# Linear attention and two mixtures of experts on one core: first k-v tails and queries behind all k and v on one queue, the four pairs in banks of their own

## The chip, the cores and the metric

One core of a Trainium2 chip runs the whole program. Its engines are TensorE (PE, with its weight loads shown as PEld), VectorE (DVE), ScalarE (ACT), GpSimd (POOL) and SyncE (SP, which here only issues transfers). The metric is the device time of one execution in microseconds; less is better. Every time below is from one profiled execution on the chip, unless it is called a median.

## What is computed

Three stages follow each other. `B, H, S, DH = 4, 8, 576, 64`, so there are 2304 rows of 512 columns after the first.

```python
kv  = einsum('bhsd,bhse->bhde', k, v)            # per batch and head, 64 x 64
out = einsum('bhsd,bhde->bhse', q, kv)
x   = out / sqrt(mean(out*out, -1) + 1e-6) * g_norm
x   = sum over 4 experts of p[:, e] * (relu(x @ w1[e]) @ w2[e])      # dense, all rows
x   = gate * (relu(x @ w1b[e]) @ w2b[e])         # 8 experts, one per row, chosen by cosine
```

## The kernel before

The work is cut into units of 384 rows (three tiles of 128 rows). Only the opening of the program is touched by the change; it computes the attention for the first unit and for the second batch's k-v product, and then the expert products of the first dense mixture start (`plain_phase`, line 1198; matmuls of line 861).

**The k-v product.** For every batch, eight heads are taken as four pairs (`NP = 4`). A pair's product accumulates over S = 576 rows: 512 of them are the main part (`MAIN`, four products of 128 rows for each head, line 127), the 64 left over are the tail (line 130). `kv_unit` (line 119) does main part and tail of a pair in one PSUM bank named by a tag, and then ScalarE copies the two 64x64 blocks into `kv_bd`, a block-diagonal form (line 133). In the opening all four pairs of batch 0 use the one bank "kv". k and v of a pair come in one transfer each of 256 KB (`load_kv`, line 137), the tails of k and v in one transfer each of 128 KB for all eight heads (`load_tail`, line 113), a query tile of 128 rows in one of 256 KB (`load_q`, line 147).

**The order of the opening** is written out by hand, from line 1043. Each engine works its own instructions in the order of the program, and each issuing engine's transfers go out in that order.

- `heat(14)` (line 1052): fourteen 128x128 products of the identity with itself. They warm TensorE and produce nothing. Each is two instructions.
- `load_tail(0, eng=nc.scalar)`: the two tails of batch 0, issued by ScalarE. Then four `issue()` calls: k and v of the four pairs, on SyncE.
- Query tiles 0, 1 and 2 (line 1062): tile 0 is issued by ScalarE, tiles 1 and 2 by SyncE.
- Behind them on SyncE's queue: the first block of expert weights (w1), the tails of batch 1, k and v of batch 1 (four pairs, into `en_b`), three more weight blocks, `dp` (the routing shares), and query tiles 3 and 4 (line 1084).
- Line 1099: for each pair `kv_unit`, `heat(2)`, and, from the third pair on, `q_first` of a query tile (four transposes at line 162 into PSUM, one copy of 128x512 by VectorE or ScalarE). After the pairs come the third `q_first` and, for each tile, `x_first`: eight products (line 179, a record for each half), a Square on ScalarE (line 1096) and a reduction on VectorE (line 1097).
- `heat(10)` (line 1108), while the root of the mean square is worked out (`rms_start`, `rms_end`). Then pairs 0 and 1 of batch 1 on TensorE, the scaling of x on VectorE (line 1118), the transposes of x (line 224) with their copies (lines 231 and 232), and pairs 2 and 3 of batch 1.
- `plain_phase` runs a list of steps with a planned length each, and beside them fillers that are due at a planned time (`todo`). In the first one, the transposes of query tile 3 (`qt_unit`, through `att([TS])`, due from 4.5) are such a filler.

Of the kernel before, what the change touches and what calls it, by code (L numbers as in the profile page):

```python
# [8 lines left out]
F32 = mybir.dt.float32  # L9
# [11 lines left out]
def attn_moe_moe_kernel(ctx: ExitStack, tc: tile.TileContext, q, k, v, g_norm, dprobs, w1, w2, emb, tau, w1b, w2b, out):  # L21
    nc = tc.nc
    ctx.enter_context(tc.manual_schedule())
    B, H, S, DH = q.shape
# [88 lines left out]
    def load_tail(b, home=None, eng=nc.sync):  # L113
        t = home if home is not None else kv_p.tile([S - MAIN, 2, H, DH], F32, name="kvtail", tag="tail", bufs=1)
        for i, src in enumerate((k, v)):
            eng.dma_start(out=t[:, i], in_=src[b, :, MAIN:S, :].rearrange("h p d -> p h d"))
        tail_raw[b] = t

    def kv_unit(b, pair, tag="kv"):
        early = b == 1  # L120
        r = en_b[:, 2 * pair:2 * pair + 2].rearrange("p i n -> p (i n)") if early else take("kv", b, pair)
        r = r.rearrange("p (i h r d) -> p i h r d", i=2, h=2, d=DH)
        tl = tail_raw[b]
        ps = psp.tile([128, DH], F32, name="pskv", tag=tag)
        for c in range(RC):
            for i in range(2):
                nc.tensor.matmul(out=ps[64 * i:64 * i + 64], lhsT=r[:, 0, i, c], rhs=r[:, 1, i, c], start=(c == 0), stop=False)
        for i in range(2):
            hd = 2 * pair + i
            nc.tensor.matmul(out=ps[64 * i:64 * i + 64], lhsT=tl[:, 0, hd], rhs=tl[:, 1, hd], start=False, stop=True)  # L130
        for i in range(2):
            sl = slice(64 * i, 64 * i + 64)
            nc.scalar.copy(kv_bd[b % 2][sl, pair, sl], ps[sl])
        if b > 1:
            issue()
# [909 lines left out]
    def heat(n, w=warm):  # L1045
        for _ in range(n):
            nc.tensor.matmul(out=w, lhsT=ident, rhs=ident, start=True, stop=True)
# [3 lines left out]

    heat(14)
    load_tail(0, eng=nc.scalar)
    for _ in range(RAW):
        issue()
    Q0 = TS

    def q_first_raw(t):
        return xr.rearrange("p u c n -> p (u c n)")[:, D * t:D * t + D]

    for t in range(Q0):
        load_q(t, nc.sync if t else nc.scalar, q_first_raw(t))
    nc.scalar.activation(out=one, in_=one, func=ACTF.Sqrt)
# [21 lines left out]
    qx = [acc[TS + t].rearrange("p (a n) -> p a n", a=NP) for t in range(Q0)]  # L1085
    px = [psp.tile([128, H, DH], F32, name=f"psx{t}", tag=("x0", "x1", "l20")[t]) for t in range(Q0)]
    ms = st_p.tile([128, TS, H], F32, name="ms3", tag="ms3", bufs=1)
# [5 lines left out]
    def x_first(t):  # L1093
# [3 lines left out]
        nc.vector.tensor_reduce(out=ms[:, t], in_=x_s[t], axis=AX.X, op=ALU.add)  # L1097

    for p in range(NP):
        kv_unit(0, p)  # L1100
        heat(2)
        if p > 1:
            q_first(p - 2)
    for t in range(Q0):
        if t + 2 < Q0:
            q_first(t + 2)
        x_first(t)
    heat(10, psp.tile([128, 128], F32, name="warm2", tag="kv"))
    ri = rms_end(*rms_start(ms, [128, TS, H], "s"))
# [3 lines left out]
    for part in range(3):  # L1113
        w1_direct(0, part, nc.gpsimd)
    for p in range(2):
        kv_unit(1, p, ("kv", "l21")[p])
    for t in range(TS):
        nc.vector.tensor_tensor(out=x_s[t], in0=px[t], in1=ri[:, t].unsqueeze(2).to_broadcast([128, H, DH]), op=ALU.mult)
    for t in range(TS):
        xt_unit(t, ("tp", "l10", "l11")[t], first=True)  # L1120
    for p in range(2, NP):
        kv_unit(1, p, ("kv", "l21")[p - 2])
    issue()
# [70 lines left out]
    todo = w2_fills(0, 0) + [(-1, f) for f in plain_direct(1)]  # L1194
    todo += [(6.0, norm_probs)]
    todo += [(14.2 + 0.4 * c, lambda c=c: nc.vector.tensor_tensor(
# [249 lines left out]
```

## Time and profile before

| what | us |
|---|---|
| median of three runs | 1115.49 |
| lowest and highest run | 1114.94, 1117.86 |
| the profiled execution, whole time | 1114.02 |
| its span in the trace | 1112.2 |
| granted TensorE clock, mean (share of full speed) | 0.999 |
| ScalarE busy in the span | 484.0 (44%) |
| VectorE busy in the span | 626.8 (56%) |

The span runs from the first to the last instruction in the trace; the whole time is 1.8 us longer. A busy time is the time in which an engine has an instruction under way; TensorE's instructions are pipelined, so several records overlap. All moments below are counted from the start of the span.

### The profile page before, as it was taken

How to read it: one execution, taken by the hardware profiler on the slowest of the kernel's cores; microseconds unless marked ns; L12 is line 12 of the kernel's file. 1: busy time of each engine (PE TensorE's matmuls, PEld its weight loads, DVE VectorE, ACT ScalarE, POOL GpSimd, SP SyncE). 2: the span in 40 equal slices, each digit the busy share in tenths (PEclk: the TensorE clock that was granted, in tenths of full speed). 3: DMA queues.
4: the chain of work that ended last, by engine and by line, in shares of the span. 5: the costliest groups of instructions: out<-in, count | busy, mean ns of one | idle time of the engine just before them, and what ended most of it. 6: DMA issues, size and time to landing. Idle time of an engine off the chain costs nothing. (4 is left out here: it accounts for less than half of the span.)

```text
span 1112.2 us, 17150 instructions
## 1 busy us (share of the span) xinstructions
PE 1098.1 (99%) x5894; PEld 965.2 (87%) x5894; DVE 626.8 (56%) x1175; ACT 484.0 (44%) x892; POOL 192.8 (17%) x232
## 2 busy tenths in 40 slices
PE   8999999999999999999999999999999999999997
PEld 8889888998888988899999888889987888888885
DVE  3665564657884455544573555743469683375452
ACT  3644437544454222233333222222366584475562
POOL 3112232321440100000020001010011121112111
PEclk9999999999999999999999999999999999999999
DMA  9736697766878446455465565465473783566471
GB/s 275 239 133 227 265 375 280 259 202 248 307 277 294 168 163 217 153 198 208 166 235 180 213 218 180 171 228 208 152 264 133 245 317 113 197 230 233 160 258 34
DMA packets 91012, 239.86 MB, mean 216 GB/s; under 512 B 19285, under 2 KB 38741, under 8 KB 90784
## 3 DMA queue, kind: packets, MB, share of 16 engines
q1 hardware_dynamic: 81376, 213.71, 54.2%
q0 software_dynamic: 7440, 24.41, 6.5%
q8 instruction: 49, 0.80, 0.3%
q10 hardware_dynamic: 2096, 0.52, 0.2%
q14 instruction: 51, 0.42, 0.1%
HBM read 230.22 MB, written 56.63 MB: 258 GB/s over the span
## 5 line engine op out<-in xcount | busy, mean ns | idle before, releaser
L968 PE MATMUL bank<-w2h,hh 128*128 128x512 f32 x576 | 227.3, 395 | 0.5 <-ACT hh L845 0.5
L968 PE MATMUL bank<-w2l,hh 128*128 128x512 f32 x576 | 225.1, 391 | 0.4 <-DMA w2l<-held_w 0.4
L968 PE MATMUL bank<-w2h,hl 128*128 128x512 f32 x576 | 225.2, 391 | 0.0
L873 PE MATMUL bank<-xth,w1h 128*128 128x384 f32 x616 | 159.6, 340 | 0.4 <-DVE acc L977 0.2
L873 PE MATMUL bank<-xtl,w1h 128*128 128x384 f32 x616 | 156.8, 335 | 0.0
L873 PE MATMUL bank<-xth,w1l 128*128 128x384 f32 x616 | 156.7, 335 | 0.0
L977 DVE SCALAR_TENSOR_TENSOR acc<-bank,dp,acc 128x512 f32<-128x512 f32 x120 | 89.8, 749 | 110.2 <-PE bank L968 110.0
L968 PEld LDWEIGHTS bank<-w2h,hl 128*128 128x128 f32 x576 | 108.1, 188 | 24.0 <-DVE hl L848 1.1
L968 PEld LDWEIGHTS bank<-w2h,hh 128*128 128x128 f32 x576 | 108.2, 188 | 22.8 <-ACT hh L845 1.8
L968 PEld LDWEIGHTS bank<-w2l,hh 128*128 128x128 f32 x576 | 108.2, 188 | 21.8 <-DMA w2l<-held_w 0.8
L873 PEld LDWEIGHTS bank<-xth,w1h 128*128 128x128 f32 x616 | 109.6, 188 | 4.0 <-ACT w1h L60 0.6
L873 PEld LDWEIGHTS bank<-xtl,w1h 128*128 128x128 f32 x616 | 111.5, 188 | 0.0
L873 PEld LDWEIGHTS bank<-xth,w1l 128*128 128x128 f32 x616 | 111.3, 188 | 0.0
L880 ACT COPY s<-bank 128x384 f32<-128x384 f32 x88 | 42.2, 479 | 156.6 <-PE bank L873 156.4
L884 POOL TENSOR_TENSOR sv<-sv,s 128x384 f32<-128x384 f32 x44 | 49.0, 1113 | 348.5 <-ACT sv L880 274.1
L61 DVE TENSOR_TENSOR w2l<-raw,w2h 128x1024 fp32r<-128x1024 f32 x64 | 75.8, 1221 | 23.6 <-ACT w2h L60 23.0
L341 DVE CUSTOM_DVE_ANT_0 scr<-row,en_b 128x512 bf16<-128x512 f32 x96 | 68.4, 713 | 10.7 <-DMA row<-x1d 9.9
L1293 PE MATMUL psy<-w2h,hth 128*128 128x512 f32 x176 | 71.0, 404 | 0.4 <-ACT hth L1284 0.4
L1293 PE MATMUL psy<-w2h,htl 128*128 128x512 f32 x176 | 68.8, 391 | 0.4 <-DVE htl L367 0.4
L1293 PE MATMUL psy<-w2l,hth 128*128 128x512 f32 x176 | 69.0, 392 | 0.0
L60 ACT CAST w2h<-raw 128x1024 fp32r<-128x1024 f32 x64 | 64.6, 1052 | 5.7 <-DMA raw<-in_moe_w_dram 5.3
L61 DVE TENSOR_TENSOR w1l<-raw,w1h 128x256 fp32r<-128x256 f32 (+2 forms) x75 | 55.0, 755 | 14.0 <-ACT w1h L60 13.9
(259 smaller groups left out, 1645.6 us busy)
## 6 DMA issues: line engine op xcount, KB each, us to landing
raw<-in_moe_w_dram SPq DMA_DIRECT2D x224, 512.0 KB
w1h<-held_w SPq DMA_DIRECT2D x28, 896.0 KB
w1l<-held_w SPq DMA_DIRECT2D x28, 896.0 KB
w2h<-held_w SPq DMA_DIRECT2D x34, 512.0 KB
w2l<-held_w SPq DMA_DIRECT2D x34, 512.0 KB
held_w<-w1h SPq DMA_DIRECT2D x16, 896.0 KB
held_w<-w1l SPq DMA_DIRECT2D x16, 896.0 KB
held_w<-w2h SPq DMA_DIRECT2D x16, 512.0 KB
```

What stands on the lines that cost most here:

```text
L60: nc.scalar.copy(hi, raw)
L61: (eng or nc.vector).tensor_tensor(out=lo, in0=raw, in1=hi.bitcast(F32), op=ALU.subtract)
L341: nc.vector.tensor_tensor_reduce(out=scr, in0=x, in1=en_b[:, e], scale=1.0, scalar=0.0, op0=ALU.mult, op1=ALU.add, accum_out=lg[:, t, e:e + 1]
L873: nc.tensor.matmul(out=ps, lhsT=wform(wo, b, w)[:, c], rhs=xform(xo, x)[:, c], start=start and n == 0, stop=(n == 5), skip_group_check=True)
L880: nc.scalar.copy(t, src)
L884: (eng or nc.vector).tensor_tensor(out=out, in0=a, in1=b, op=ALU.add)
L968: nc.tensor.matmul(out=ps, lhsT=h_t[o][f][u][:, ns], rhs=w[j][:, a], start=(k == 0 and m == 0), stop=(k == 3 and m == 2))
L977: nc.vector.scalar_tensor_tensor(out=fin, in0=ps, scalar=dp[:, t, e:e + 1], in1=ac, op0=ALU.mult, op1=ALU.add)
L1293: nc.tensor.matmul(out=ps, lhsT=x[:, f], rhs=w[j][:, o], start=(f == 0 and i == 0), stop=(f == NF - 1 and i == 2))
```

## The change

Both tails of batch 0 and query tile 0 are issued by SyncE, behind all k and v of batch 0. The main parts of the four pairs are computed one after the other, each in a bank of its own, with a `heat` behind each; the four tails, and the copies, follow them, with the copies of pairs 2 and 3 on VectorE. The query tiles' transposes come after that, and the x products of a tile start before the transposes of the next-but-one. There is less warm-up work: 5 in place of 14 at the start, 7 and 1 in place of 8 around the pairs, 4 in place of 10 after x. Pairs 0 and 1 of batch 1 share one bank with a `heat(2)` between them, and pair 3 of batch 1 becomes a filler of the first expert phase, due at 2.1.

```diff
-    def kv_unit(b, pair, tag="kv"):
+    def kv_main(b, pair, tag):
         early = b == 1
         r = en_b[:, 2 * pair:2 * pair + 2].rearrange("p i n -> p (i n)") if early else take("kv", b, pair)
         r = r.rearrange("p (i h r d) -> p i h r d", i=2, h=2, d=DH)
-        tl = tail_raw[b]
         ps = psp.tile([128, DH], F32, name="pskv", tag=tag)
         for c in range(RC):
             for i in range(2):
                 nc.tensor.matmul(out=ps[64 * i:64 * i + 64], lhsT=r[:, 0, i, c], rhs=r[:, 1, i, c], start=(c == 0), stop=False)
+        return ps
+
+    def kv_rest(b, pair, ps, copy=nc.scalar.copy):
+        tl = tail_raw[b]
         for i in range(2):
             hd = 2 * pair + i
             nc.tensor.matmul(out=ps[64 * i:64 * i + 64], lhsT=tl[:, 0, hd], rhs=tl[:, 1, hd], start=False, stop=True)
         for i in range(2):
             sl = slice(64 * i, 64 * i + 64)
-            nc.scalar.copy(kv_bd[b % 2][sl, pair, sl], ps[sl])
+            copy(kv_bd[b % 2][sl, pair, sl], ps[sl])
+
+    def kv_unit(b, pair, tag="kv"):
+        kv_rest(b, pair, kv_main(b, pair, tag))
         if b > 1:
             issue()
...
-    heat(14)
-    load_tail(0, eng=nc.scalar)
+    heat(5)
     for _ in range(RAW):
         issue()
+    load_tail(0)
     Q0 = TS
...
     for t in range(Q0):
-        load_q(t, nc.sync if t else nc.scalar, q_first_raw(t))
+        load_q(t, nc.sync, q_first_raw(t))
...
-    px = [psp.tile([128, H, DH], F32, name=f"psx{t}", tag=("x0", "x1", "l20")[t]) for t in range(Q0)]
...
+    mains = []
     for p in range(NP):
-        kv_unit(0, p)
-        heat(2)
-        if p > 1:
-            q_first(p - 2)
+        mains.append(kv_main(0, p, ("kv", "x0", "x1", "l20")[p]))
+        heat(2 if p + 1 < NP else 1)
+    for p in range(NP):
+        kv_rest(0, p, mains[p], nc.scalar.copy if p < 2 else nc.vector.tensor_copy)
+    px = [psp.tile([128, H, DH], F32, name=f"psx{t}", tag=("x0", "x1", "l20")[t]) for t in range(Q0)]
+    q_first(0)
+    heat(1)
     for t in range(Q0):
-        if t + 2 < Q0:
-            q_first(t + 2)
+        if t + 1 < Q0:
+            q_first(t + 1)
         x_first(t)
-    heat(10, psp.tile([128, 128], F32, name="warm2", tag="kv"))
+    heat(4, psp.tile([128, 128], F32, name="warm2", tag="kv"))
...
-    for p in range(2):
-        kv_unit(1, p, ("kv", "l21")[p])
+    kv_unit(1, 0, "kv")
+    heat(2, psp.tile([128, 128], F32, name="warm2", tag="l21"))
+    kv_unit(1, 1, "kv")
...
-    for p in range(2, NP):
-        kv_unit(1, p, ("kv", "l21")[p - 2])
+    kv_unit(1, 2, "kv")
     issue()
...
-    todo += [(6.0, norm_probs)]
+    todo += [(2.1, lambda: kv_unit(1, 3)), (6.0, norm_probs)]
```

## Rows read from the trace of the kernel before

A row of the timeline gives start, length, engine, line, operation, what it writes and reads, and how many instructions were merged; in brackets stands the idle time before them and what ended it.

**Rows 1.** The page's head and its busy time of each engine.

```profile
span 1112.2 us, 17150 instructions
PE 1098.1 (99%) x5894; PEld 965.2 (87%) x5894; DVE 626.8 (56%) x1175; ACT 484.0 (44%) x892; POOL 192.8 (17%) x232
```

**Rows 2.** Waits of TensorE after 25 us: total, times, longest.

```profile
PE psm L1271 <- DVEq L807: 2.2, 2, 2.0
PE bank L968 <- ACT hh L845: 0.5, 2, 0.4
```

**Rows 3.** Timeline of TensorE in the first 26 us.

```profile
9.48 0.69 PE L127 MATMUL pskv<-raw 128*64 128x64 f32 x16 [1.33 <-DMA raw<-in_v_dram]
10.10 0.33 PE L130 MATMUL pskv<-kvtail 64*64 64x64 f32 x4
10.36 0.71 PE L1047 MATMUL warm<-ident 128*128 128x128 f32 x4
...
14.48 1.04 PE L162 MATMUL psq<-ident,xr 128*128 128x128 f32 x8
15.36 2.84 PE L179 MATMUL psx<-kvbd,acc 128*128 128x128 f32 x24
18.04 2.40 PE L1047 MATMUL warm<-ident 128*128 128x128 f32 x20
...
21.37 0.69 PE L127 MATMUL pskv<-en_b 128*64 128x64 f32 x16
...
22.25 1.55 PE L224 MATMUL psxt<-ident,acc 128*128 128x128 f32 x12
...
25.48 0.97 PE L861 MATMUL bank<-xth,w1h 128*128 128x384 f32 x4
```

**Rows 4.** Timeline of the queues of ScalarE and SyncE: when each transfer is issued.

```profile
0.76 0.71 ACTq L116 DMA_DIRECT2D kvtail<-in_k_dram  x1
...
0.76 0.46 SPq L139 DMA_DIRECT2D raw<-in_k_dram  x1
...
7.06 2.79 SPq L154 DMA_DIRECT2D xr<-in_q_dram  x2
9.96 2.38 SPq L614 DMA_DIRECT2D raw<-in_moe_w_dram  x1
```

**Rows 5.** Windows: PE, PEld, DVE, ACT, POOL busy; PEclk, DMA share, GB/s.

```profile
2.00:5.00 3.00, 3.00 (x16) 3.00 (x16) 0.00 (x0) 1.49 (x2) 1.50 (x3) 1.00 0.98 261
5.00:8.00 3.00, 2.93 (x37) 2.59 (x36) 0.00 (x0) 0.38 (x2) 0.00 (x0) 1.00 0.91 225
8.00:12.00 4.00, 2.64 (x47) 2.08 (x45) 0.00 (x0) 0.45 (x3) 0.00 (x0) 1.00 1.12 349
14.00:20.00 6.00, 6.00 (x55) 6.00 (x55) 2.81 (x5) 3.20 (x8) 0.00 (x0) 1.00 0.97 280
```

**Rows 6.** DMA queues from 5 to 8, 8 to 12 and 12 to 14 us.

```profile
q1 hardware_dynamic: 452, 0.44, 51.3%
q10 hardware_dynamic: 945, 0.24, 39.0%
...
q1 hardware_dynamic: 2082, 1.32, 103.7%
...
DMA packets 1295, 0.46 MB, mean 229 GB/s; under 512 B 1123, under 2 KB 1295, under 8 KB 1295
```

**Rows 7.** Timeline of TensorE's weight loads: transposes of query tile 3.

```profile
32.04 0.42 PEld L162 LDWEIGHTS psq<-ident,qraw 128*128 128x128 f32 x4 [0.37 <-DMA qraw<-in_q_dram]
```

**Rows 8.** Timeline of VectorE: first query copy, and the scaling of x.

```profile
13.17 0.69 DVE L1091 COPY acc<-psq 128x512 f32<-128x512 f32 x1 [12.25 <-PE psq L162]
...
21.20 1.89 DVE L1118 TENSOR_TENSOR acc<-psx,rs 128x512 f32<-128x512 f32 x3
```

**Rows 9.** Timeline of ScalarE: copies of the transposed x.

```profile
22.94 1.84 ACT L231 ACTIVATE xth<-psxt,g 128x512 fp32r<-128x512 f32 x3 [0.15 <-PE psxt L224]
```

**Rows 10.** The warm-up products before 5 us and from 5 to 6.5 us.

```profile
L1047 PE MATMUL warm<-ident x16: 418/421/582, 1.4 to 4.7; 128*128 128x128 f32 x16
L1047 PE MATMUL warm<-ident x11: 275/275/275, 5.1 to 6.2; 128*128 128x128 f32 x11
```

## The prediction

> **What bounds the kernel now.** I read the page first, for which engine fills the span: TensorE is busy 1098.1 of 1112.2 us [rows 1]. Almost every TensorE instruction is therefore on the path, and a change can win only idle time or filler. The waits of TensorE after 25 us come next: the longest is 2.0 us in the late routing, and the six other lines have 0.2 to 0.5 us each, the one of the second row the most [rows 2]. So what can be won lies in the first 25.5 us, before the expert products start, and I went through that stretch with TensorE's timeline [rows 3]. The reader should see that pair 1 of batch 0 waits 1.33 us for its v, and that from 9.48 us the stream has hardly a gap until the first expert product at 25.48; but 2.4 us of it (from 18.04) is warm-up, and so is 0.71 us behind each pair.
>
> The work in that stretch is paced by loads. SyncE's queue goes out in order, and the ACT queue carries the k and v tails and the first query tile beside it [rows 4]. The DMA windows show 225 GB/s while both queues move data (5 to 8 us), 349 where almost only SyncE's does (8 to 12), and 229 where most packets are under 512 B (12 to 14) [rows 5, 6]. One more wait matters: at 32.04 us the transposes of the fourth query tile have waited 0.37 us for their load [rows 7]. It stands behind everything above on SyncE's queue. Whatever the opening wins must pass this load.
>
> **The change, part by part.** The sum is made against the profiled execution, 1114.02 us (span 1112.2), which is 1.47 below the median of the runs, 1115.49.
>
> *Order of loads.* The bytes up to the third query tile stay the same: 2.10 MB of k and v, 0.26 of tails, 0.79 of queries, 3.15 MB together. What may change is how fast they move. Between 5 and 8 us the ACT queue moved 0.24 MB of small packets and SyncE's 0.44 MB of larger ones in 3 us [rows 6]. Done one after the other, 0.24 MB at 229 GB/s is 1.05 us and 0.44 MB at 349 is 1.26 us: 2.3 us, a gain of 0.7. I call this gain g. Its low end is 0, if only the order changes. Its high end is 1.8: 0.68 MB at 349 is 1.95 us (gain 1.06), and the 0.78 MB of 2 to 5 us at 349 instead of 261 is 2.24 us (gain 0.76), though the ramp of the first load lies in there. I take 0.7, because it charges small packets their own row. On SyncE's queue three issues are added ahead of the second query tile and all behind it; the first, the longest of the three on ACT, takes 0.71 us there. I cost them at nothing, since the queue's issue of the third query tile ended at 9.85 us (7.06 plus 2.79) [rows 4] and its bytes were moving until 13 us. If that cover is gone, they cost 3 x 0.71 = 2.1 us (a rival below).
>
> By the Trainium skill ("DMA: Bandwidth & Descriptors", section "Issuing engines are not separate DMA queues") transfers of all issuing engines share the same 16 DMA engines and interleave, so moving them to another queue saves only issue time. By that rule g would be 0, and the sum with it; the 225 beside the 349 GB/s speaks against it as the whole story.
>
> *Main products.* Four pairs in banks of their own drop the wait of the next pair for ACT's copies, which lay beside the heat of 0.71 us. The main part of a pair takes 0.62 us (9.48 to 10.10), a heat of two 0.45 (four records, 0.112 us apart as the twenty that take 2.40 us with the last one's 0.275), together 1.07, while 0.52 MB at 349 GB/s brings a pair every 1.5 us. They are hidden behind the loads. The first pair can start when it lands instead of after heat: also hidden, since the queries end this stage.
>
> *Tails, queries, x products.* Four tails cost 4 x 0.26 = 1.04 us (10.10 to 10.36), a tile's four transposes 0.44 (half of 14.48 to 15.36), a tile's x products 0.89 (a third of 15.36 to 18.04) [rows 3]. When did the third query tile land? Its bytes had passed by 13.3 us (2.86 MB by 12 us, the rest at 229 GB/s), and by 14.92 its transposes ran without a gap. I take 14.5, near the late end, because a landing trails its bytes; changed, 13.8. Queries of 0.26 MB land 1.15 us apart, so the second lands at 12.65: transposes to 13.1, x products of tile 0 to 14.0, transposes of tile 2 to 14.4, x products of tiles 1 and 2 to 16.2. Its copy on VectorE (0.69 us [rows 8]) lies beside tile 1's products. The x products so end 1.8 us sooner than at 18.04. The copies of pairs 2 and 3 go to VectorE, idle there until 13.17 [rows 8]: nothing.
>
> *Where that gain goes.* The 3.16 us from the end of x to the scaling at 21.20 [rows 8] stay, so scaling could start at 19.4. But what is late next is batch 1. The transposes of x stand behind its pair 1 on TensorE. Bytes up to pair 1 of batch 1: 3.15 + 0.52 (first weight block) + 0.26 + 1.05 = 4.98 MB; the windows have moved 5.0 MB by 20.0 us (0.01 before 2 us, then 0.78, 0.68, 1.39, 0.46 and 6 us of 280 GB/s) [rows 5, 6]. Landed: between 20.0 and 21.37, where its products started unhindered. I take 21.0 (the lag of the queries), changed 20.3. Then 0.88 us for the pair gives 21.2; transposes to 22.7; pair 2 to 23.55; ACT's three copies start 0.7 us behind the first transpose and take 1.84 [rows 9], ready at 23.75. The first expert product moves from 25.48 to 23.75: 1.73. Pair 3, moved into the phase, gives 0.88 back: 0.85 stays.
>
> *The fourth query tile.* TensorE gets there at 31.67 - 0.85 = 30.8; the load, if it shifts by g, lands at 32.04 - 0.7 = 31.3. So the net gain is **g, 0.7 us**, and the wait there grows from 0.37 to about 0.5. With g = 0 the products start at 24.45, 0.15 stays, and the wait swallows it: 0. The heat that is dropped (9 of 14 at the start, 6 of 10 after x) and the two added in batch 1 (0.45 us) count nothing besides; they fill waits for loads. POOL's queue is not touched, and its subtractions for the weights begin earlier with the scaling. Behind 32 us only small waits are left [rows 2] to eat any of it.
>
> Sum: 1114.02 - 0.7 = 1113.3 for a run like the profiled one, 1115.49 - 0.7 = **1114.8** for the median.
>
> **The rivals.** (a) Only the order changes, g = 0, the wait at 32 us takes all of it: **1115.5**. For: same bytes, a DMA share above 0.9 in every window read. Against: the 225 GB/s. (b) g is 1.8, since one queue also runs better from 2 to 5 us: **1113.7**. Against: the ramp at the start would have to shrink too. (c) Slower: SyncE cannot issue fast enough. Three more issues delay all loads behind them by 2.1 us if issue time sets the landings: **1117.6**. For: the issue of the first weight block took 2.38 us and ended at 12.34. Against: its queue had 349 GB/s going at the time. It decides from the point where the third query tile's issue ends behind its data. (d) Slower by more: the clock. The warm-up products last 421 ns each until about 5 us and 275 after it [rows 10], when TensorE had run them without a gap from 1.4 us on; the granted clock in the windows reads 1.00 all the while [rows 5], so I read the change as one from 1.2 to 2.4 GHz by the durations alone. With five products instead of fourteen TensorE stops before it has risen. If the lower level held until the expert products, every step from the second query tile on would double: x products end at 19.8, four heats at 21.6, pairs 0 and 1 of batch 1 with their heat at 26.0, transposes at 28.6, pair 2 at 30.3, which is 4.8 us behind 25.48; with 0.88 for pair 3, and the wait of 0.37 gone, 5.3 us: **1120.8**. Against: at the lower level a pair and its heat take 2.1 us, more than the 1.5 us of its loads, so TensorE would again be without a gap, and rise as it did before; until the queries land this costs nothing. The Trainium skill ("TensorE: Matmul & The Clock Gate", Part 1) has the throttled clock as the default that activity releases; that is the same rise, and agrees with rows 10.
>
> **How the numbers follow.** Forecast 0.52, (a) 0.28, (b) 0.10, (c) 0.06, (d) 0.04. About 0.3%, or 3.3 us, is what a measurement of this kernel can tell from no change; only (d), or a stray median, reaches it. So faster 0.02, same 0.94, slower 0.04. Range: down to (b) for a run like the profiled one, 1112.2; up to (a) plus half of the 2.4 us to the highest run, 1116.7.
>
> **What would show it.** Right: pair 3's main products start before 10 us, x products end near 16.2, first expert product near 23.8, the wait of the fourth query tile is 0.4 to 0.6 us at about 31.3. Wrong: that tile still starts at 32.0 (a), or after 33 (c); heat or x products show 421 ns behind 10 us (d); or the first pair of batch 1 no longer waits, so that the load is not what ends the stage.

## The result, and the profile after

The changed kernel takes **1121.63 us** (median of six runs, 1120.84 to 1124.06) where the kernel before, on the same chip, takes 1116.64 (six runs, 1114.94 to 1117.88): ratio **1.0054** (95% interval 1.0042 to 1.0067). It is slower by 0.5%, outside the range given and on the side that had been given 0.04. The prediction's sum stood on 1115.49, the median of three of these six runs of the kernel before. The profiled executions stand at 1121.86 and 1114.02, their spans at 1119.9 and 1112.2, 7.7 us apart: more than the medians, so the two profiles exaggerate the loss by some 2.7 us.

The page of the changed kernel, head and busy time, against [rows 1]:

```profile
span 1119.9 us, 17097 instructions
PE 1098.0 (98%) x5868; PEld 964.0 (86%) x5868; DVE 627.5 (56%) x1179; ACT 483.3 (43%) x888; POOL 193.2 (17%) x232
```

TensorE is busy as long as before, though 26 of its instructions are gone: the 13 warm-up products that the change saves. In part that is because products at the lower level of the clock, shown below, last longer. So the whole 7.7 us stand as idle time. TensorE's timeline of the opening, against [rows 3]:

```profile
1.38 2.50 PE L1053 MATMUL warm<-ident 128*128 128x128 f32 x10 [1.38 <-POOL ident masks.py:199]
4.42 0.99 PE L126 MATMUL pskv<-raw 128*64 128x64 f32 x16 [0.54 <-DMA raw<-in_v_dram]
...
8.73 1.12 PE L126 MATMUL pskv<-raw 128*64 128x64 f32 x16 [2.69 <-DMA raw<-in_v_dram]
9.79 1.22 PE L1053 MATMUL warm<-ident 128*128 128x128 f32 x4
10.94 1.12 PE L126 MATMUL pskv<-raw 128*64 128x64 f32 x16
...
14.13 0.68 PE L133 MATMUL pskv<-kvtail 64*64 64x64 f32 x16 [0.39 <-DMA kvtail<-in_v_dram]
15.04 0.66 PE L168 MATMUL psq<-ident,xr 128*128 128x128 f32 x4 [0.23 <-DMA xr<-in_q_dram]
16.25 0.66 PE L168 MATMUL psq<-ident,xr 128*128 128x128 f32 x4 [0.32 <-DMA xr<-in_q_dram]
...
19.80 1.16 PE L185 MATMUL psx<-kvbd,acc 128*128 128x128 f32 x8 [0.68 <-DVE acc L1096]
20.80 1.06 PE L1053 MATMUL warm<-ident 128*128 128x128 f32 x8
23.40 0.69 PE L126 MATMUL pskv<-en_b 128*64 128x64 f32 x16 [1.54 <-DMA en_b<-in_v_dram]
...
24.92 0.69 PE L126 MATMUL pskv<-en_b 128*64 128x64 f32 x16
...
28.77 0.94 PE L867 MATMUL bank<-xth,w1h 128*128 128x384 f32 x4 [0.57 <-ACT kvbd L136]
31.05 0.69 PE L126 MATMUL pskv<-en_b 128*64 128x64 f32 x16
```

The reader should see three things. The loads are late: the tails start 14.13, the second query tile 16.25, and pair 0 of batch 1 waits 1.54 us for its v, so that pair 1 starts at 24.92 where it started at 21.37. A pair takes 1.12 us where it took 0.69, which is the lower level of TensorE's clock, 1.2 of 2.4 GHz. And the first expert product comes at 28.77, **3.29 us later** than at 25.48. The windows, against [rows 5] (PE, PEld, DVE, ACT, POOL busy; PEclk, DMA share, GB/s):

```profile
2.00:5.00 3.00, 2.46 (x20) 2.20 (x21) 0.00 (x0) 0.24 (x2) 1.51 (x3) 1.00 0.82 256
5.00:8.00 3.00, 1.05 (x15) 0.79 (x11) 0.00 (x0) 0.00 (x0) 0.00 (x0) 1.00 0.61 155
8.00:12.00 4.00, 3.27 (x37) 2.84 (x37) 0.00 (x0) 0.00 (x0) 0.00 (x0) 0.57 1.17 290
12.00:14.00 2.00, 1.74 (x24) 1.36 (x22) 0.00 (x0) 0.00 (x0) 0.00 (x0) 1.00 1.36 142
14.00:20.00 6.00, 4.64 (x47) 4.15 (x48) 3.07 (x8) 2.61 (x7) 0.00 (x0) 1.00 1.20 245
```

From 2 to 20 us that is 0.77, 0.47, 1.16, 0.28 and 1.47 MB, 4.15 together; before it was 4.99 MB [rows 5, 6]. The 0.84 MB that are missing take 2.3 us at the 372 GB/s that the kernel before reaches from 20 to 26 us. So the loads, which were to come sooner, come over two microseconds later. The 155 GB/s between 5 and 8 us are a quarter of that (0.21 MB); 0.41 MB more are lost from 8 to 14 us, where tails and queries now follow in a row, and 0.21 behind. From 8 to 12 us the granted clock reads 0.57, after TensorE has waited 2.69 us.

The rest of the difference is lost far behind the opening. TensorE's waits in 85 to 100 us and in 296 to 320 us, changed kernel:

```profile
97.12 0.47 PE L974 MATMUL bank<-w2h,hh 128*128 128x512 f32 x1 [0.58 <-DMA w2h<-held_w]
98.24 0.50 PE L974 MATMUL bank<-w2l,hh 128*128 128x512 f32 x1 [0.65 <-DMA w2l<-held_w]
...
309.11 0.59 PE L879 MATMUL bank<-xth,w1h 128*128 128x384 f32 x2 [1.35 <-DVE acc L983]
```

and the same places in the kernel before:

```profile
92.98 0.50 PE L968 MATMUL bank<-w2l,hh 128*128 128x512 f32 x1 [0.38 <-DMA w2l<-held_w]
...
302.71 0.58 PE L873 MATMUL bank<-xth,w1h 128*128 128x384 f32 x2 [0.24 <-DVE acc L977]
```

The lag of the changed kernel is 98.24 - 92.98 = 5.26 us at the first place and 309.11 - 302.71 = 6.40 at the second, after 3.29 at the first expert product. So about 2 us are lost between 28 and 98 us (pair 3 as a filler and two waits for w2) and 1.1 between there and 309 us. Of the 1.3 us lost behind that, 1.0 is a fall of the clock near 868 us, changed kernel and then kernel before:

```profile
868.35 0.53 PE L1280 MATMUL psm<-w1h,xgl 128*128 128x512 f32 x1 [1.95 <-DVEq L813]
...
870.39 0.63 PE L1280 MATMUL psm<-w1l,xgh 128*128 128x512 f32 x1
```

```profile
862.03 0.50 PE L1271 MATMUL psm<-w1h,xgl 128*128 128x512 f32 x1 [1.97 <-DVEq L807]
...
863.99 0.39 PE L1271 MATMUL psm<-w1l,xgh 128*128 128x512 f32 x1
```

Both wait 2 us there. Behind the wait the granted clock reads 0.67 (868 to 870 us) and 0.50 (870 to 872) in the changed kernel, and 1.00 in the kernel before. The same fall shows in ten of the 18 profiles of this study, whatever their edit; what decides on it is not known.

### The profile page after: what moved, and what is told of

It reads as the page before. It is cut to its first block, busy times and chain, and to the rows that moved or that the text cites. A ratio compares the mean times of both kernels' runs of the same rounds, so it can differ in the third digit from the quotient of the medians.

```text
span 1119.9 us, 17097 instructions
## 1 busy us (share of the span) xinstructions
PE 1098.0 (98%) x5868; PEld 964.0 (86%) x5868; DVE 627.5 (56%) x1179; ACT 483.3 (43%) x888; POOL 193.2 (17%) x232
```

## The experiments

The theories at the start. **L**: the loads' order alone makes the loss. **C**: the clock's lower level does, because fewer warm-up products stand at the start. **G**: the two loads of g_norm, 128 elements of four bytes on GpSimd's queue, slow down all loads that run beside them, and the change puts k and v, on which everything waits, there. **I**: 13 products fewer move the moments at which the program's own code is fetched, and one fetch falls on the w2 loads near 95 us. Later **S**: weight stores near 292 us get in the way of a row load. Each group of experiments has runs of the kernel before beside it; a ratio is always to those, and it is not the quotient of two medians.

### e1: the loads back on ScalarE's queue

The changed kernel with tails and query tile 0 issued as before.

```diff
+    load_tail(0, eng=nc.scalar)
...
-    load_tail(0)
...
-        load_q(t, nc.sync, q_first_raw(t))
+        load_q(t, nc.sync if t else nc.scalar, q_first_raw(t))
```

> The changed kernel with its loads alone put back: both tails and query tile 0 on ScalarE's queue ahead of everything, the rest as changed. Theory L (the order of the loads on one queue is what costs): transposes of the third query tile start by 15 us instead of 17.6, first expert product at 25.5 or sooner instead of 28.8, time about 1117 (4 to 5 us less than the changed kernel's 1121.6). Rival O (the new order of TensorE's work, the shorter warm-up or the moved pair 3 costs): it stays at 1120 or above.

Measured: 1121.69 us, ratio 1.0046 (1.0026 to 1.0066). The loads move again as before (228 GB/s from 5 to 8 us), but pair 1 waits 1.97 us, all main parts but the last take 1.12, and the first expert product comes at 28.93. Undoing the order of loads alone gives nothing back, so L alone is refuted.

### e2: the loads' order alone

The kernel before with its tails and query tile 0 on SyncE's queue behind all k and v (the mirror of e1's edit).

> The kernel before with the order of the loads alone changed: tails and query tile 0 on SyncE's queue behind all k and v, TensorE's work as before. Theory L: about 1120 to 1121, first expert product 3 us later than before (28 to 29 us). Rival O: within 1 us of the kernel before (1116.6).

Measured: 1124.09 us, ratio 1.0063 (1.0041 to 1.0085). TensorE's timeline:

```profile
14.38 0.48 PE L130 MATMUL pskv<-kvtail 64*64 64x64 f32 x4 [7.15 <-DMA kvtail<-in_v_dram]
...
15.94 1.12 PE L127 MATMUL pskv<-raw 128*64 128x64 f32 x16
```

In the old order of products, the first pair's tail holds TensorE for 7.15 us, and then everything piles up at the lower level (granted 0.53 from 12 to 14 us). The first expert product comes 9.1 us late, at 34.58. The new order of products is what makes the new order of loads bearable. And late losses do not follow from being late: this kernel, which has the instructions of before, waits 0.4 us for w2, as before, and has no wait near 309 us.

### e3: fourteen warm-up products again

```diff
-    heat(5)
+    heat(14)
```

> The changed kernel with fourteen warm-up products at the start again instead of five. Theory C (TensorE at half its clock from 8 to 12 us costs): granted clock 1.00 in that stretch, first expert product 1 to 3 us sooner, time 1119 to 1120. Theory L: the main products of pairs 1 and 2 get shorter (0.69 instead of 1.12 us) but nothing behind the tails moves; 1121.6 within 0.7 us.

Measured: 1120.59 us, ratio 1.0036 (1.0021 to 1.005). The main parts take 0.69 again, but the clock falls later, once the tails have kept TensorE waiting:

```profile
12.68 0.69 PE L126 MATMUL pskv<-raw 128*64 128x64 f32 x16 [1.05 <-DMA raw<-in_v_dram]
13.30 0.49 PE L1053 MATMUL warm<-ident 128*128 128x128 f32 x2
14.77 1.12 PE L133 MATMUL pskv<-kvtail 64*64 64x64 f32 x16 [0.98 <-DMA kvtail<-in_v_dram]
```

x products end past 22.9 us, first expert product 30.13. A start at full clock is not enough, so C as stated falls too.

### e8 and e9: both undone, and the clock held by hand

e8 is e1 and e3 together; e9 is the changed kernel with 14 warm-up products at the start and more in every wait up to the x products.

> The changed kernel with the old order of loads and fourteen warm-up products as well: only TensorE's new order behind the start is left. Theory LC (two causes, each enough by itself: the loads land later, and TensorE falls to half its clock when it waits for them): all main products take 0.69 us, x products end at 17 to 18 us, first expert product at 25 to 26, time within 1 us of the kernel before, against 4.6 per mille more with either undone alone. Rival O (the new order costs by itself, by the copies of query tiles behind the reductions on VectorE, 0.55 and 0.67 us): x products end at 19 or later and 1118 or more.

> The changed kernel with the loads as changed, and warm-up products in every wait up to the x products (14 at the start, 4 behind a pair, 12 behind pair 3, more between the query tiles), so that TensorE keeps its clock. Theory LC: main products 0.69 us and x products of a tile 0.9 us all along, but the third query tile still lands at 17 us: x products end near 19.5 to 20, first expert product near 28, 1119 to 1121. Rival C (the clock is the whole loss): first expert product by 26 us, 1117 or less.

e8: 1121.17 us, ratio 1.0051 (1.0032 to 1.007). e9: 1122.53 us, ratio 1.0056 (1.0041 to 1.0071). e8's timeline:

```profile
6.06 0.69 PE L126 MATMUL pskv<-raw 128*64 128x64 f32 x16
6.67 0.71 PE L1053 MATMUL warm<-ident 128*128 128x128 f32 x4
9.80 0.69 PE L126 MATMUL pskv<-raw 128*64 128x64 f32 x16 [2.42 <-DMA raw<-in_v_dram]
10.42 0.71 PE L1053 MATMUL warm<-ident 128*128 128x128 f32 x4
11.26 1.12 PE L126 MATMUL pskv<-raw 128*64 128x64 f32 x16
```

With the loads and the warm-up of before, this profile still loses the clock, and what theory LC expected does not come. The wait for pair 1 is 2.42 us where it was 1.33 [rows 3], and behind it the granted clock reads 0.50 (12 to 14 us). Of the 1.09 us more, 0.41 are the place of the tail that stood between pairs 0 and 1 and has moved; the rest is that pair 0 started 0.36 us sooner and the load of pair 1 came 0.32 later, which the edit does not explain. The signs of rival O came: x products end at 21.55, and TensorE waits 0.56 and 0.68 us for copies of query tiles on VectorE. In e9 the clock is held at the full level throughout, at the price of warm-up in the way of the queries (transposes at 17.46 and 19.02): first expert product 30.83. Holding the clock is not worth what it costs here.

### e4: pair 3 of batch 1 back ahead of the expert products

```diff
+    kv_unit(1, 3, "l21")
...
-    todo += [(2.1, lambda: kv_unit(1, 3)), (6.0, norm_probs)]
+    todo += [(6.0, norm_probs)]
```

> The changed kernel with pair 3 of batch 1 back ahead of the first expert product instead of in its phase. Theory F (the filler costs its own 0.9 us, because TensorE waited 0.57 us ahead of the expert products anyway): 0.5 us less than the changed kernel, first expert product 0.3 us later. Theory L: at most that. If the filler disturbs the phase behind it, 1 us or more is won.

Measured: 1121.35 us, ratio 1.0045 (1.003 to 1.0059), within the changed kernel's interval. The first expert product comes at 28.93, only 0.16 later, though 0.88 us of work stand ahead of it again: in the changed kernel TensorE waits 0.57 there anyway for ScalarE's copy. At 33 us it is 0.9 ahead of the changed kernel. The filler therefore does not move work off the path, it uncovers a wait.

### e5: g_norm later

```diff
+    gate_g = st_p.tile([128, 1], F32, name="gateg", tag="gateg", bufs=1)
+    nc.gpsimd.tensor_copy(gate_g, q_first_raw(0)[:, 0:1])
```

ahead of the two loads of g_norm, so that GpSimd issues them when query tile 0 has landed.

> The changed kernel with the two small loads of g_norm (64 values of 4 bytes each, on GpSimd's queue) issued only after query tile 0 has landed, instead of at 2.2 us. Theory G (these loads hold up the sixteen DMA engines from about 5 to 8 us, where 155 GB/s were moved): 250 GB/s or more in that stretch, v of pair 1 landed near 7 instead of 8.6 us, all loads behind it about 1 us sooner, time 1120 to 1121. Rival (the dip comes from elsewhere, such as the ramp of the first loads): below 200 GB/s from 5 to 8 us again, and no change of time.

Measured: 1119.59 us, ratio 1.0033 (1.0021 to 1.0045). The windows (columns as above):

```profile
5.00:8.00 3.00, 1.95 (x32) 1.66 (x30) 0.00 (x0) 0.00 (x0) 0.00 (x0) 1.00 0.99 315
8.00:12.00 4.00, 3.08 (x51) 2.46 (x51) 0.00 (x0) 0.00 (x0) 0.00 (x0) 1.00 1.29 242
```

315 GB/s where the changed kernel had 155, with the same transfers on SyncE's queue. The only other traffic there was g_norm's, as the DMA queues of the changed kernel from 5 to 8 us show (packets, MB, share of 16 engines):

```profile
q1 hardware_dynamic: 478, 0.46, 60.6%
q0 software_dynamic: 39, 0.00, 0.8%
```

It is 39 packets with next to no bytes, and 0.8% of the engines' time by the record. How much is lost beside it differs between executions: with g_norm's loads early, the six profiles with this order of loads moved 154 to 218 GB/s from 5 to 8 us (the changed kernel, e2, e3, e4, e9, e16); with them late, the four moved 315 to 362 (e5, e10, e14, e15). Pair 1 now starts at 7.04, the main parts behind the first take 0.69, the granted clock is 1.00, the first expert product comes at 25.81. The 2.96 us gained there are 2.1 per mille, 2.3 us, in the time.

### e13: g_norm by ScalarE at the start

The two loads issued by ScalarE instead.

> The changed kernel with the loads of g_norm issued by ScalarE at the start instead of by GpSimd. Theory G1 (GpSimd's queue is what slows the engines): no dip, 280 GB/s or more from 5 to 8 us, pair 1 starts by 7.5 us, time like that of the run with the late g loads (1119.6). Theory G2 (loads of 4-byte pieces slow the engines from any queue): the dip moves up to 2 to 5 us (below 220 GB/s there), pair 0 starts after 5 us, time 1120 to 1122.

Measured: 1119.3 us, ratio 1.003 (1.002 to 1.004). From 2 to 5 us the loads now move at 219 GB/s (256 before this edit) and from 5 to 8 at 323: the slow stretch goes with g_norm's loads, to where they now are. The main parts run at the lower level until 12.5 us and the first expert product is at 28.18, yet the time is that of e5. So 2.4 us of opening more do not show in this median. The two profiled executions do differ, 1120.21 and 1118.37 us, e13's above its median and e5's below; why the medians agree stays open.

### e7: g_norm later in the kernel before

> The kernel before with the loads of g_norm issued after query tile 0 has landed. Theory G: more than the 225 GB/s of before from 5 to 8 us, pair 1 starts before 9 us, the wait for query tile 3 at 32 us and all in front of it moves up by 0.5 to 1 us, time 0.5 to 1 us below the kernel before. Rival: nothing moves, within 0.3 us.

Measured: 1114.64 us, ratio 0.9983 (0.9972 to 0.9995). The kernel before gains from it too, though its profile shows little of it in the opening (277 GB/s from 5 to 8 us, first expert product at 25.37). Its k and v were perhaps partly spared, as 0.24 MB of what moved beside g_norm were tails and a query tile. Part of what it gains lies in the longest runs: its lowest run is 0.8 us below the lowest of the kernel before (1113.21, 1113.99), its highest 5.4 us below the highest (1115.06, 1120.51), and all runs of the kernel before above 1117 us have a mean granted clock of 0.995 or 0.996. Where the clock falls in those, no kept profile shows.

### e10 and e11: thirteen warm-up products more, thirteen fewer

e10 is e5 with 14 at the start and 8 behind x, so that TensorE has the 5894 instructions of before. e11 is the kernel before with 13 fewer (11 at the start, none behind pairs 2 and 3, 4 behind x).

> The changed kernel with the loads of g_norm late and thirteen warm-up products added where TensorE waits (fourteen at the start, eight after x), which brings its count of instructions up to the next expert stages to that of the kernel before. Theory I (a 16 KB fetch of TensorE's instructions, which the count moves from 83 to 92 us in the run with the late g loads, holds up a DMA engine while the second set of w2 is fetched): the fetch falls before 87 us, the waits for w2 near 95 us sum to 0.5 us or less instead of 1.4, and the run near 306 us loses less than 0.8; time 1.0 to 2.0 us under that of the run with the late g loads alone. Rival (these late losses come from the shift in time or from chance): they stay, 1119 to 1120.

> The kernel before with thirteen warm-up products fewer (11 of 14 at the start, none behind pairs 2 and 3, 4 of 10 after x) and nothing else. Theory I: the first expert product is no later than before (25.5 us or sooner), but the instruction fetch of TensorE moves from 83 to 88 us or later, into the fetch of w2, and 0.5 to 2.5 us are lost behind 90 us: 1116 to 1118. Rival: within 0.5 us of the kernel before, or faster.

e10: 1117.73 us, ratio 1.0014 (1.0005 to 1.0023). e11: 1120.19 us, ratio 1.0032 (1.0018 to 1.0046). TensorE's waits between 90 and 98 us, e5 and then e10:

```profile
94.24 0.47 PE L974 MATMUL bank<-w2h,hh 128*128 128x512 f32 x1 [0.75 <-ACT w1h L60]
95.36 0.50 PE L974 MATMUL bank<-w2l,hh 128*128 128x512 f32 x1 [0.66 <-DMA w2l<-held_w]
```

```profile
93.68 0.50 PE L974 MATMUL bank<-w2l,hh 128*128 128x512 f32 x1 [0.20 <-DMA w2l<-held_w]
```

1.41 us of waiting become 0.20 when 13 products that compute nothing are added over 70 us earlier, and e11, with 13 taken from the kernel before, gets 0.81 and 0.65 there. What stands beside it is the fetch of code on a DMA queue of its own, `q8 instruction`. In the changed kernel it falls between 94 and 96 us, in e5 and e11 between 90 and 92, in the midst of the w2 loads; in the kernel before, e7 and e10 between 82 and 84, ahead of them:

```profile
q1 hardware_dynamic: 763, 2.39, 99.5%
q8 instruction: 1, 0.02, 0.9%
```

(the changed kernel, DMA queues from 90 to 96 us). Two more kernels stand between: e3 and e8 have nine of the thirteen products back, the fetch comes 0.8 us ahead of the first issue of a w2 load (89.3 and 90.14 us, 87.8 and 88.59), and the waits are 0.66 and 2.32 us; with all thirteen it comes 1.3 to 1.8 us ahead. That the number of warm-up products decides is shown by e5 and e10, whose openings are 0.29 us apart, and e11 agrees; that it acts through this fetch is what the rows suggest.

e11 was to leave the opening as it was, and did not. Pair 0's tail waited 1.24 us and pair 1 another 0.84, and then the clock fell (granted 0.65 from 8 to 12, 0.50 from 12 to 14), and the first expert product came at 27.32, 1.84 late. In e7, with all fourteen products at the start, the same tail waited 1.51 us and pair 1 still took 0.69. So the warm-up of the kernel before is not only filler: with less of it the clock goes.

### e12: the kernel before, tuned by what had been seen

g_norm late, no heat behind pair 3, x products of tile 0 ahead of the transposes of tile 2, 12 warm-up products behind x, query tiles 3 and 4 loaded ahead of `dp`, which is normalized later.

> A try at a version that beats both, from the kernel before: g_norm late, no warm-up behind pair 3, x products of tile 0 ahead of the transposes of tile 2 with the copy of tile 2 ahead of the reduction of tile 0 on VectorE, twelve warm-up products after x, query tiles 3 and 4 loaded ahead of the routing shares, and these normalized at 8.5 instead of 6.0. Expected: x products end at 17.3 instead of 18.0 us, no wait for query tile 3 at 32 us, 0.5 to 1.0 us under the kernel before with the late g loads (1114.6); if the first expert product is held by pair 1 of batch 1 all the same, only the 0.4 us of that wait.

Measured: 1115.02 us, ratio 0.9985 (0.9976 to 0.9995), no better than e7. x products ended at 17.81, 0.23 sooner than before, but pair 3 of batch 1 waited 0.30 us for its load and the first expert product came at 26.05, 0.57 later.

### e14, e15, e16: the weight stores near 292 us

Until here the loss near 309 us (TensorE waits 0.7 to 1.6 us there in ten kernels) was open. There GpSimd waits for the store of a finished row of x (`x1d`) and loads it back (`row`); VectorE waits for the row, and the `acc` that TensorE needs stands behind that on VectorE. In the kernel before, GpSimd waits 2.71 us for the store, in the changed one 5.45. In all 14 profiles two stores of weights (`held_w<-w1h`, `held_w<-w1l`, line 68) are issued by SyncE near that store: over 1 us after it where the wait is 2.7 us (before, e2, e7, e12), 0.10 to 0.14 us after it in the ten where it is 3.9 to 6.3. The edit puts them behind the next k and v loads:

```diff
-        return [((10.4, 19.1)[n % 2], lambda: w1_sums(e, n))] + spread(w1_fills(e, n), *((13, 21), (23, 30))[n % 2])
+        fs = spread(w1_fills(e, n), *((13, 21), (23, 30))[n % 2])
+        if p == 1 and n == 0:
+            fs[3] = (26, fs[3][1])
+        return [((10.4, 19.1)[n % 2], lambda: w1_sums(e, n))] + fs
```

e14 is e10 with it, e15 is e14 with pair 3 put back as in e4, e16 is the changed kernel with it.

> The kernel of e10 (changed kernel, g_norm late, 13 warm-up products more), with one edit at 292 us: the two stores of the first weight forms of the next pair of units (held_w<-w1h, held_w<-w1l) stand on SyncE's queue behind the next k and v loads instead of ahead of them. Theory S (the row load of GpSimd waits 3.88 us in e10 and 2.71 before because these stores are issued 0.14 us after the x1d store that it waits for, and 1.24 us after it before): with the stores gone from there, GpSimd's wait is 2.7 us or less, TensorE's wait for acc near 304 us falls from 1.01 to 0.5 or less, time 1117.0 to 1117.3 (ratio 1.0008 to 1.0012). Rival F (the wait comes from where in the program that stretch is reached, or from chance): GpSimd's wait stays at 3.7 to 5.5, TensorE's at about 1.0, time 1117.7.

> The kernel of e14, with pair 3 of batch 1 back ahead of the first expert product. If the list of losses is complete (loads under the g_norm loads, instruction count, stores at 292 us, pair 3 as a filler), nothing of the change's loss is left beyond the opening itself: first expert product at 25.6 to 26.4, no 0.85 us lost near 31 us, time 1115.9 to 1116.7 (ratio 0.9995 to 1.0005). If something else costs, it stays at 1117 or more (1.0010 or more).

> The changed kernel with the edit of e14 alone. Theory S: GpSimd's wait for the x1d store falls from 5.45 to 2.7 or less, TensorE's wait near 309 us from 1.35 to 0.5 or less, time 1120.7 (1.0 us less than the changed kernel's 1121.6, ratio 1.0045). Rival F: 5 us, 1.3 us, 1121.6 (1.0054).

e14: 1115.86 us, ratio 0.9996 (0.9983 to 1.0008). e15: 1115.2 us, ratio 0.9983 (0.9972 to 0.9995). e16: 1119.01 us, ratio 1.002 (1.0006 to 1.0034). All three gain more than was expected, e16 3.4 per mille on the changed kernel where 0.9 had been. Part of that is not the edit's: e16's profile, with the same opening as the changed kernel, had 218 GB/s from 5 to 8 us instead of 155 and its first expert product at 27.72 instead of 28.77, so executions differ there without any edit. TensorE's wait goes (0.23 us in e16, none in e14). But not as theory S had it: GpSimd's wait for the store stays at 3.78 in e14 and 5.04 in e16. What gets shorter is the whole way from the issue of the store to VectorE's first use of the row. GpSimd and VectorE, changed kernel, then e14:

```profile
296.39 0.58 POOL L986 DMA_DIRECT2D x1d<-acc  x1 [5.33 <-DVE acc L983]
...
306.34 0.70 DVE L347 CUSTOM_DVE_ANT_0 scr<-row,en_b 128x512 bf16<-128x512 f32 x1 [4.86 <-DMA row<-x1d]
```

```profile
292.60 0.59 POOL L989 DMA_DIRECT2D x1d<-acc  x1 [5.33 <-DVE acc L986]
...
300.39 1.20 DVE L347 CUSTOM_DVE_ANT_0 scr<-row,en_b 128x512 bf16<-128x512 f32 x1 [2.69 <-DMA x1d<-acc]
```

9.95 us in the changed kernel, 7.79 in e14; 8.80 in e16 (295.31 to 304.11), 8.83 in the kernel before (291.11 to 299.94), 9.60 in e10. So the stores cost 1.1 to 1.8 us on this way, on store and load together. Why they are issued 0.14 us behind the x1d store in one kernel and 1.24 behind it in another is only partly known: SyncE's issue of the v load ahead of them takes 0.47 us in the ten kernels and 1.5 to 1.7 in the four.

### e17: the kernel before with both findings

e7 with the edit of e14.

> The kernel before, with g_norm's loads late (as in e7) and the two weight stores of 292 us behind the next k and v loads (as in e14). If the stores lengthen the way from the x1d store to its row in the kernel before too (8.8 us from the issue of the store to VectorE's first use of the row; 7.8 in e14), it falls to about 7.8 us, the waits of TensorE for acc near 303 us (0.24 in the kernel before, 0.49 in e7) go, and the time is 1114.0 to 1114.4 where e7 stood at 1114.6 (ratio 0.9976 to 0.9980 on e7's 0.9983). If the stores cost only where they run into the x1d store, as in the changed kernel, nothing moves: 8.8 us and 0.9983.

Measured: 1113.33 us, ratio **0.9971** (0.996 to 0.9982), the fastest kernel of this study. The way from store to row is 7.34 us (290.31 to 297.65), and TensorE shows no wait there. In this profile pair 1 starts at 8.72 us where it started at 9.48 [rows 3], and all behind it comes sooner as well: the first expert product starts at 24.78, 0.70 before that of the kernel before.

### The list of losses

| kernel | ratio | interval |
|---|---|---|
| the change | 1.0054 | 1.0042 to 1.0067 |
| + g_norm late (e5) | 1.0033 | 1.0021 to 1.0045 |
| + 13 warm-up products more (e10) | 1.0014 | 1.0005 to 1.0023 |
| + weight stores late (e14) | 0.9996 | 0.9983 to 1.0008 |
| + pair 3 of batch 1 ahead of the expert products (e15) | 0.9983 | 0.9972 to 0.9995 |
| before, g_norm late, weight stores late (e17) | 0.9971 | 0.996 to 0.9982 |

Each step is worth 1.3 to 2.1 per mille. The intervals of neighbouring rows overlap, and the rows have different runs of the kernel before beside them, so the size of a single step is loose, that of pair 3 above all; the way from the first row to e15 is clear. With all four the change's own opening may still stand 1.2 per mille, 1.3 us, behind the old one given the same two (e17), but the intervals of the last two rows overlap. The profiles point the same way, with the first expert product at 27.20 in e15 and 24.78 in e17, though e10 and e14, whose openings are the same, differ by 0.83 themselves (25.52, 26.35).

## Why the prediction was wrong

**The gain g of the loads' order (0.7 us, 0 to 1.8 as the bounds): the step that failed.** I read the 225 GB/s from 5 to 8 us as the price of two queues with small packets, and charged the small packets their own row, 229. The runs show another price in that stretch: g_norm's loads. They were in the trace of before, on GpSimd's queue, and I did not count them, as they hold next to no bytes (kernel before, DMA queues from 5 to 8 us):

```profile
q0 software_dynamic: 47, 0.00, 1.1%
```

The change did not touch them; it put k and v under them, 155 GB/s instead of 225. Small packets in a row did not do as charged either. With g_norm out of the way (e10) packets of 256 bytes move at 217 GB/s from 12 to 13 us, and from 10 to 11 us as this row shows:

```profile
DMA packets 689, 0.17 MB, mean 175 GB/s; under 512 B 689, under 2 KB 689, under 8 KB 689
```

At 175 GB/s 0.26 MB, the size of the tails, take 1.5 us where the 229 had 1.1. The second query tile, which I had landing at 12.65 us, holds up its transposes until 16.25 in the changed kernel, and with g_norm out of the way until 13.44 in e10 and 14.84 in e15. The line of e10:

```profile
13.44 0.66 PE L168 MATMUL psq<-ident,xr 128*128 128x128 f32 x4 [0.31 <-DMA xr<-in_q_dram]
```

What g measured follows from windows of a quarter of a microsecond, summed up: the first 3.15 MB have moved by 13.4 us in the kernel before and by 16.1 in the changed one, a loss of 2.7 us where I had a gain of 0.7. With g_norm late on both sides they have moved by 12.8 to 13.3 us in the old order (e7, e12, e17) and by 13.4 to 14.4 in the new one (e5, e10, e14, e15). So most of the loss is g_norm's, and the new order by itself gains nothing and loses up to 1.6 us. The bound below zero was missing: I had closed the range at 0 because "only the order changes", without asking what else runs in the stretch into which each load moves.

The rule of the Trainium skill cited in the prediction ("DMA: Bandwidth & Descriptors", section "Issuing engines are not separate DMA queues") would have had g at 0. Of the runs with g_norm late, e10 is near to that (13.4 us beside 13.1 in e7), and e14 and e15 are not (14.2 and 14.4).

**The clock, rival (d): right in kind, wrong in when.** I gave it 0.04, because "at the lower level a pair and its heat take 2.1 us, more than the 1.5 us of its loads, so TensorE would again be without a gap". But the pairs did not come every 1.5 us: pair 1 came 2.69 us after the work of pair 0 was done, and then the granted clock was 0.57. In that profile the clock had risen during pair 0 (0.99 us, its heat 0.71) and fell again. In e4 and e16, with the same five products at the start, pair 0 took 1.12 us, its heat 1.22 and pair 1 again 1.12: there it had not risen at all, just as (d) has it. e8 and e11 show a fall after 2.42 and after 1.24 and 0.84 us of waiting, and e3 shows it for the tails. "Until the queries land this costs nothing" holds in part: in the changed kernel and in e13 the second query tile still holds TensorE up (0.32 and 0.18 us), but in e1, e8 and e16 TensorE waits for no load between pair 1 and the x products, so there the lower level sets the pace. The 1120.8 that I gave for (d) lies near the result by luck, as its terms are others: x products did not run at half speed and end at 19.8, they ran at the full level (1.06 for a tile) and ended at 20.8, behind late loads and late main parts.

**The copy of the third query tile "lies beside tile 1's products": wrong.** On VectorE it stands behind the reduction of tile 0, which waits for ScalarE's Square:

```profile
18.46 0.69 DVE L1102 TENSOR_REDUCE ms<-acc 128x8 f32<-128x512 f32 x1 [2.00 <-ACT acc L1101]
19.07 0.68 DVE L1096 COPY acc<-psq 128x512 f32<-128x512 f32 x1
```

TensorE waits 0.68 us for it, and 0.67 or 0.68 in e1, e5, e10 and e14. So x products end at 17.99 in e10, where the clock was at its full level, and not at 16.2: of the 1.8 us, 0.68 is this wait and 0.8 the third tile's transposes, at 14.82 where I had 14.0. That is as late as before, 18.04 [rows 3]; this gain, too, was none.

**What is late next: right.** Batch 1 does set the end of the opening: its pair 0 waits 1.54 us for its load in the changed kernel. From the start of pair 1 to the expert products it is 3.85 us (24.92 to 28.77), and 4.11 before (21.37 to 25.48), where pair 3 took 0.88 of them: with it gone I had 3.23, and the wait of 0.57 for ScalarE's copy makes up most of the rest.

**Pair 3 as a filler "gives 0.88 back":** the lag grew by 1.07 at that place (3.29 to 4.36), and the wait of 0.37 for query tile 3 went, as the tile landed in time for a later TensorE. But taking it out of the opening bought only 0.16 (e4), since the wait for the copy was under it.

**"The heat that is dropped counts nothing besides": wrong twice.** 13 products fewer cost 1.2 us of waiting near 95 us by their number alone (e5 against e10; 1.1 in e11 against the kernel before), and the heat in the opening holds the clock (e11).

**"Behind 32 us only small waits are left": true of the kernel before, and no bound for the changed one.** Some 3.6 us of the profiled difference arise there (4.07 us of lag behind the fourth query tile, 7.7 at the end): the waits for w2, the wait near 309 us and the fall of the clock near 868. The waits are small because the transfers fall just so; with a shift of a few microseconds, or of 13 products, the w2 loads stand beside a code fetch and the row load beside weight stores. e2 shows that lateness by itself does not do it.

**The other rivals.** (c), SyncE too slow in issuing, is not what happened: its third query tile was issued until 13.3 us (7.46 plus 5.82 for the three), 2.8 us before its bytes had moved. The check that I had named failed at its first row (pair 3's main products start at 12.63 us, not before 10). Of the signs of a wrong forecast, the one for (c) came without its cause, as the fourth query tile starts at 36.19, and the one for (d) at the edge, as a heat of two products behind pair 1 took 1.22 us from 9.79 (0.71 at the full level). "The first pair of batch 1 no longer waits" did not come: it waited for a load that was late.

## What to carry to other kernels

When loads are reordered, list what else moves in the stretch into which each of them goes, tiny loads on other queues first: with two loads of 256 bytes each beside them, loads ran at 154 to 218 GB/s for three microseconds and not at 315 to 362, and moving them (or the weight stores away from a store whose row is waited for) was worth more than the whole reordering. An operation is hidden only if its place on its own engine's queue is, so read what stands ahead of it there. And in a kernel that is 99% busy, warm-up and filler instructions are part of the timing: count what is dropped, and look at the late waits as well as at the stretch that is edited.

## What the runs showed of the hardware that I had not expected

- 128 elements of four bytes, loaded by GpSimd, held SyncE's loads beside them to 155 GB/s from 5 to 8 us (154 to 218 in six profiles); without them the same loads ran at 315 (e5; 315 to 362 in four). Issued by ScalarE at the start, they took the slow stretch to 2 to 5 us, 219 GB/s (e13).
- Loads of 256-byte packets ran at 175 GB/s from 10 to 11 us and at 217 from 12 to 13 (e10). That the slower stretch is the tails', which lie on 64 partitions where a query tile lies on 128, is not shown.
- Thirteen products of no use, dropped, cost 1.2 us over 70 us later; beside it stands a code fetch that comes at 94 to 96 us instead of 82 to 84 (e5, e10 and e11 for the number).
- Main parts of a pair took 1.12 us, the lower level of the clock, in the changed kernel and in e1, e2, e4, e8, e11, e13 and e16; in e11 with nothing changed but the warm-up. They took 0.69 wherever g_norm's loads came late behind 14 warm-up products (e7, e10, e12, e14, e15, e17), and but for the first of them behind five (e5).
- The granted clock of the windows does not always say so: in e1 it reads 1.00 from 8 to 12 us, where two pairs took 1.12 us each. The durations of equal products are the safer sign.
- The clock fell behind a wait of 1.95 us at 868 us in the changed kernel and not behind one of 1.97 at 862 us in the kernel before; it cost 1.0 us.
